# An adaLN attention and feed-forward block: a written-out table of steps for the first iterations, q taken first, scales by pointer, row sums on POOL, a staged passage to the feed forward

## The chip, the cores and the metric

The kernel runs on one core of a Trainium2 chip. A core has a matrix engine (TensorE, PE in the profile, its weight loads PEld), three elementwise engines (VectorE or DVE, ScalarE or ACT, GpSimd or POOL), and a queue engine (SyncE or SP) that issues the DMAs here. Each engine takes its instructions in program order and waits on semaphores for what the others produce. The metric is device time in microseconds, the median of several executions.

## What is computed

One transformer block with its modulation taken from a condition vector, in f32 inputs and outputs: 2048 rows of 512, 32 heads of 128, each attending to the last 512 rows of its cache, and a gated feed forward of width 1376.

```python
mod = (silu(c) @ w_mod).reshape(1, 6, 1, -1)       # sa, ca, ga, sb, cb, gb
h = layernorm(x) * (1 + ca) + sa
q = (h @ wq) per head; scores = q k^T * Dh**-0.5; o = softmax(scores) v   # k, v: last 512 rows
x = x + ga * (o @ wo)
h = layernorm(x) * (1 + cb) + sb
x = x + gb * ((gelu(h @ w_gate) * (h @ w_up)) @ w_down)
```

## The kernel before

Every f32 operand of a large product is split in a high and a low f16 part, and each product is made of three matmuls (high by high, high by low, low by high) that add up in one PSUM bank. So that f16 holds them, operands are scaled by their largest magnitude: `h_max` takes the maximum of a weight or cache tile on DVE (L239), `cross_a` and `cross_b` (L108, L117) bring it to all partitions with a transpose and a matmul, `h_scale` multiplies on POOL (L319) and `in_two` (L321) writes the high part on ACT and the low part on POOL. For some tiles `h_high` (ACT, L308) and `h_low` (DVE, L313) do both steps at once. `h_scalars` (L249) multiplies the inverse scales of a head, [128 x 1] each, into the factor of the exponential (L254, for wq and k) and the factor of the output (L257, for v and wo).

Queries come in 4 groups of 512 rows, heads in 16 groups of 2, which gives 128 iterations `it` of one head and one query group; 8 of them share two heads. The main loop `slot(i)` (L825) is a pipeline over iterations, written out in Python: slot i issues the scores of iteration i (`s_mm`, L440 to L442), its maxima (`s_max`, L448), exponentials (`s_exp`, ACT, L459 with the f16 copy L462), low parts and transposing DMAs (`s_low`, POOL L467 and SP L472), the value product of iteration i-2 (`pv`, L487 to L489), its evacuation (`o_high` L493, `o_low` L496) and the output product of iteration i-3 with its addition into `acc` (`wo_mm` L503, `wo_add` L515). A slot has two halves, and everything else is hung into named places of the halves: `at(half, f, ...)` puts a call in a list, and `hooks(half)` issues the list. Halves are counted 2i and 2i+1; n + 0.25 stands behind the first score product, n + 0.5 behind the maxima, n at the end of the first half, n + 1.25, n + 1.5 and n + 1 likewise in the second. `QS` holds the q products and `EV` their evacuation `q_high` (ACT, L428) and `q_low` (DVE, L431) out of the single PSUM bank psQ, issued one half slot later.

From head group 3 on q is made by a Strassen-like scheme of seven products for eight (`w_product`, L395), for which the normalised rows are added and subtracted: `t_full` (L357) adds high and low part to an f32 tile again, `t_sum` (L363) subtracts on POOL, `t_split` (L366) splits the result. Those steps are hung at halves 8 to 34.

Ahead of the loop (L544 to L613) the first query group is normalised: row statistics (`ln_stats`, DVE, with the reciprocal root by a power on POOL), the affine step on ACT (`ln_norm` L148), transposes on PE (`ln_pe` L160). `ln1_split` (L527) applies the modulation columns `cols` on the way out of PSUM and splits. The columns come from w_mod by eight DVE instructions and column matmuls (L554 to L561). `warm(n)` issues n transposes of the identity into an unused bank. The later three query groups are normalised and split in slots 0 to 3, by `ln_norm` and `ln1_chunk` hooks (L630 to L655), with the first heads' v and wo between them.

At the end of the loop `ff_cross` and `ff_scalars` (L792, L804) make the scales of the feed forward, `x1_mul` and `x1_add` form x + ga * attention of the first query group on POOL, `ln2_*` normalise it, and `fill` issues pieces of the first feed-forward products between the last slots. After the loop the feed forward runs over 4 query groups by 11 column tiles.

Tiles come from rings of named buffers: `raw` has 8, `h32` 3, `p32` 2, `q` 3; PSUM has one bank each for psO and psQ, two for psW and two pairs for the scores.

## Time and profile before

| | before |
|---|---|
| median of 3 runs | 1811.05 us (1810.65 to 1814.49) |
| profiled execution, its own time | 1813.38 us |
| span in that profile | 1811.6 us |
| mean granted TensorE clock | 0.984 |
| busy: PE, DVE, ACT, POOL | 95%, 72%, 59%, 58% |

The span runs from the first to the last instruction of the trace. A row of the timeline reads: start and duration in us, engine, line, operation, output and inputs with their shapes, how many, and in square brackets how long the engine idled before and on whom it waited. A row of the waits reads: who waits for whom, us in total, number of times, the longest. A row of a table of stretches reads: from and to, length, and for each engine busy us and instructions, then the granted clock, the share of DMA and GB/s. A row of groups reads: busy us and mean ns, then the idle time before the group; with three numbers and slashes it is minimum, median and maximum ns.

### The profile page before, as it was taken

What the parts mean: (1) busy time and instruction counts of PE and PEld (TensorE: products, weight loads), DVE (VectorE), ACT (ScalarE), POOL (GpSimd) and SP (SyncE); (2) the same over time, 40 slices, a digit from 0 to 9 for tenths busy, and PEclk for the clock granted to TensorE, in tenths of its full rate; (3) what the DMA queues carried; (4) which work ended last, traced back from release to release, by engine and by line L of the source; (5) the groups of instructions that cost most, each with busy time, mean ns of one, the idle gap of its engine ahead of it and who ended that gap; (6) DMA issues with size and microseconds to landing.
All of it is one profiled execution on the core that took longest, in us unless ns stands there. A gap on an engine that the chain in (4) does not pass through costs nothing. (4 is left out here: it accounts for less than half of the span.)

```text
span 1811.6 us, 23734 instructions
## 1 busy us (share of the span) xinstructions
PE 1721.7 (95%) x7950; PEld 790.7 (44%) x7950; DVE 1307.3 (72%) x2480; ACT 1077.1 (59%) x2016; POOL 1051.8 (58%) x826
## 2 busy tenths in 40 slices
PE   8688989999999999999999999999799899999998
PEld 5233434444444444444444444444344344444443
DVE  6678887878788888888887888888787746424222
ACT  3656757776767777776767676667577534121211
POOL 2557878687867767776767677676568800101010
PEclk8799999999999999999999999999999999999999
DMA  6346667687878777777768786767577731101000
GB/s 197 82 100 111 134 111 146 134 152 137 172 128 161 131 153 137 150 132 151 142 134 164 131 164 133 152 133 140 99 134 156 130 99 43 47 0 47 1 24 24
DMA packets 658954, 213.55 MB, mean 118 GB/s; under 512 B 580304, under 2 KB 640720, under 8 KB 658832
## 3 DMA queue, kind: packets, MB, share of 16 engines
q1 hardware_dynamic: 658832, 212.03, 58.6%
q8 instruction: 63, 1.03, 0.2%
q14 instruction: 59, 0.48, 0.1%
HBM read 65.14 MB, written 4.19 MB: 38 GB/s over the span
## 5 line engine op out<-in xcount | busy, mean ns | idle before, releaser
L467 POOL TENSOR_TENSOR pp<-p,pp 128x1024 f16<-128x1024 f32 x256 | 546.3, 2134 | 378.6 <-ACT pp L462 287.7
L459 ACT ACTIVATE p<-psS,st,es 128x512 f32<-128x512 f32 x512 | 393.2, 773 | 287.3 <-DVE st L450 279.6
L515 DVE SCALAR_TENSOR_TENSOR acc<-psW,st,acc 128x512 f32<-128x512 f32 x496 | 365.3, 741 | 24.1 <-PE psW L505 23.8
L448 DVE TENSOR_REDUCE st<-psS 128x2 f32<-128x1024 f32 x256 | 311.0, 1215 | 28.1 <-PE psS L442 27.1
L462 ACT ACTIVATE pp<-p 128x1024 f16<-128x1024 f32 x256 | 270.6, 1057 | 8.1
L503 PE MATMUL psW<-wo,oT 128*128 128x512 f16 x512 | 195.0, 381 | 23.5 <-DVE acc L515 22.1
L489 PE MATMUL psO<-pT,v 128*128 128x512 f16 x512 | 195.0, 381 | 5.7 <-POOL v L323 5.7
L440 PE MATMUL psS<-kT,q 128*128 128x512 f16 x512 | 197.2, 385 | 0.2 <-DMA kT<-k 0.2
L441 PE MATMUL psS<-kT,q 128*128 128x512 f16 x512 | 196.6, 384 | 0.0
L487 PE MATMUL psO<-pT,v 128*128 128x512 f16 x512 | 194.6, 380 | 2.0 <-ACT v L322 1.4
L442 PE MATMUL psS<-kT,q 128*128 128x512 f16 x512 | 196.3, 383 | 0.0
L504 PE MATMUL psW<-wo,oT 128*128 128x512 f16 x512 | 195.0, 381 | 0.0
L505 PE MATMUL psW<-wo,oT 128*128 128x512 f16 x512 | 194.6, 380 | 0.0
L488 PE MATMUL psO<-pT,v 128*128 128x512 f16 x512 | 194.6, 380 | 0.0
L1000 DVE SCALAR_TENSOR_TENSOR gl<-psS,ffs,gl 128x512 f32<-128x512 f32 (+1 forms) x44 | 33.0, 750 | 180.1 <-ACT gl L999 180.1
L999 ACT ACTIVATE gl<-psS,ffs 128x512 f32<-128x512 f32 (+1 forms) x44 | 30.2, 687 | 222.8 <-PE psS L989 222.8
L496 DVE SCALAR_TENSOR_TENSOR oT<-psO,oT 128x512 f16<-128x512 f32 x128 | 88.0, 687 | 40.2 <-ACT oT L493 39.9
L403 PE MATMUL psQ<-T,S 128*128 128x512 f16 x468 | 113.7, 379 | 2.9 <-DVE q L431 2.4
L239 DVE TENSOR_REDUCE mx<-raw 128x1 f32<-128x512 f32 x128 | 86.5, 679 | 41.5 <-DMA raw<-in_A_wq_dram 25.9
L493 ACT ACTIVATE oT<-psO 128x512 f16<-128x512 f32 x128 | 75.5, 590 | 58.5 <-PE psO L489 57.8
L459 ACT ACTIVATION_READ_ACCUMULATOR p<-psS,st,es 128x1 f32 x512 | 100.2, 196 | 0.0
L431 DVE SCALAR_TENSOR_TENSOR q<-psQ,q 128x512 f16<-128x512 f32 x49 | 33.7, 688 | 89.2 <-ACT q L428 89.2
(262 smaller groups left out, 3088.1 us busy)
## 6 DMA issues: line engine op xcount, KB each, us to landing
raw<-in_A_wq_dram SPq DMA_DIRECT2D x32, 256.0 KB, 3.3
raw<-in_A_k_cache_dram SPq DMA_DIRECT2D x32, 256.0 KB, 3.4
raw<-in_A_v_cache_dram SPq DMA_DIRECT2D x32, 256.0 KB, 3.4
...
pT<-pp SPq DMA_TRANSPOSE x512, 3.2
...
```

The source lines that it names most:

```text
L440: nc.tensor.matmul(p[:, j, :], q[:, 0, qs], k[:, 0, :], start=True, stop=False)
L441: nc.tensor.matmul(p[:, j, :], q[:, 0, qs], k[:, 1, :], start=False, stop=False)
L442: nc.tensor.matmul(p[:, j, :], q[:, 1, qs], k[:, 0, :], start=False, stop=True)
L448: nc.vector.tensor_reduce(st[:, 2 * b:2 * b + 2], PSS[it, b], op=OP.max, axis=AX.X, negate=True)
L459: nc.scalar.activation(p32[:, j, :], p[:, j, :], AF.Exp, bias=st[:, n:n + 1], scale=ES[head_qg(it)[0]][:, 0:1], accum_out=st[:, 4 + n:5 + n])
L462: nc.scalar.activation(pp[:, :, 0, :], p32, AF.Copy)
L467: nc.gpsimd.tensor_tensor(pp[:, :, 1, :], p32, pp[:, :, 0, :], op=OP.subtract)
L487: nc.tensor.matmul(po, vh, pT[:, t, :], start=(t == 0), stop=False)
L489: nc.tensor.matmul(po, v[:, 1, t * P:(t + 1) * P], pT[:, t, :], start=False, stop=(t == 3))
L503: nc.tensor.matmul(p, o[:, 0, ts], w[:, 0, :], start=True, stop=False)
L504: nc.tensor.matmul(p, o[:, 0, ts], w[:, 1, :], start=False, stop=False)
L515: nc.vector.scalar_tensor_tensor(a, p, r, a, op0=OP.mult, op1=OP.add)
```

## The change

The hooks and straight code of the beginning are replaced by one table, `PLAN`: each entry has a place (-1 for ahead of the loop, else a half), a step's name and its arguments. For `norm` and `chunk` the engine stands in the entry. In `slot`, `run(EV, ...)` moves ahead of the hooks of n + 0.25 and n + 1.25. In the setup the modulation sums come before the normalisation, the warm-up is 54 transposes and those between are gone; the two steps that make `cols` and its scale are taken apart. The negated mean times the root is formed by two POOL instructions when a group's statistics are complete. `h_scalars` and the feed forward's scalar steps use tensor_scalar with a pointer operand where they used scalar_tensor_tensor or tensor_tensor. The sums of `t_full` all run on POOL, and their order in the halves is new. The first head group's later loads and splits (`EARLY`) have other halves. At the end the scalar batch is cut in four, a memset moves to the setup, the scaling of gb moves to ACT, and the steps of the first feed-forward rows are hung one by one.

```diff
+PLAN = (
+    (-1, "stats", 1, 0), (-1, "stats", 1, 1), (-1, "max", "first", 0), (-1, "cols_add"), (-1, "cols_bound"),
+    (-1, "max", "first", 1), (-1, "warm", 0), (-1, "cols_scale"), (-1, "cross", "first", "a"),
+    (-1, "cross", "first", "b"), (-1, "stats", 1, 2), (-1, "chunk", 0, 0, "", "S", "Y"), (-1, "s_scale"),
+    (-1, "chunk", 0, 2, "", "V", "V"), (-1, "scalars", 0, "qk"), (-1, "high", "k", 0), (-1, "high", "wq", 0),
+    (-1, "chunk", 0, 1, "", "S", "Y"), (-1, "low", "wq", 0), (-1, "max", "second", 0),
+    (-1, "chunk", 0, 3, "", "S", "V"), (-1, "q", 0), (-1, "low", "k", 0), (-1, "turn", 0), (-1, "q_high", 0),
+    (-1, "max", "second", 1), (-1, "stats", 1, 3), (-1, "warm", 0), (-1, "cross", "second", "a"), (-1, "warm", 0),
+    (-1, "cross", "second", "b"), (-1, "warm", 0), (-1, "q_low", 0), (0.25, "norm", 1, 1, "V"),
+    (0.25, "high", "wq", 1), (0.25, "low", "wq", 1), (0.25, "high", "k", 1), (0.5, "norm", 1, 3, "S"),
+    (0.5, "norm", 1, 2, "S"), (0.5, "norm", 1, 0, "V"), (0, "low", "k", 1), (0, "q", 1), (0, "max", "later", 2),
+    (1.25, "q_high", 1), (1.25, "max", "later", 3), (1.25, "max", "later", 1),
+    (1.25, "chunk", 1, 1, "psW", "S", "Y"), (1.25, "q_low", 1), (1.5, "scalars", 1, "qk"), (1.5, "turn", 1),
+    (1.5, "chunk", 1, 3, "psO", "S", "Y"), (1.5, "chunk", 1, 0, "psQ", "V", "V"), (1.5, "stats", 2, 0),
+    (1.5, "stats", 2, 1), (1.5, "chunk", 1, 2, "psO", "S", "V"), (1.5, "stats", 2, 2), (1, "stats", 2, 3),
+    (1, "max", "later", 0), (1, "stats", 3, 0), (2.25, "cross", "later", "a"), (2.25, "norm", 2, 2, "V"),
+    (2.25, "norm", 2, 3, "S"), (2.25, "cross", "later", "b"), (2.5, "norm", 2, 0, "S"), (2.5, "scale", "v", 0),
+    (2.5, "scale", "wo", 0), (2.5, "norm", 2, 1, "V"), (2, "stats", 3, 1), (2, "chunk", 2, 0, "psO", "S", "Y"),
+    (2, "stats", 3, 2), (3.5, "chunk", 2, 1, "psW", "V", "V"), (3.5, "split", "v", 0), (3, "scalars", 0, "vo"),
+    (3, "stats", 3, 3), (4.25, "chunk", 2, 2, "psW", "V", "Y"), (4.25, "high", "v", 1), (4.5, "split", "wo", 0),
+    (4.5, "chunk", 2, 3, "psW", "S", "Y"), (4, "norm", 3, 2, "V"), (4, "norm", 3, 1, "S"), (5.5, "norm", 3, 0, "S"),
+    (5, "norm", 3, 3, "V"), (5, "chunk", 3, 1, "psW", "S", "Y"), (5, "low", "v", 1), (6.25, "scale", "wo", 1),
+    (6.25, "scalars", 1, "vo"), (6.25, "chunk", 3, 0, "psW", "S", "Y"), (6.5, "chunk", 3, 2, "psW", "S", "Y"),
+    (6, "split", "wo", 1), (7.5, "chunk", 3, 3, "psW", "V", "V"),
+)
+EARLY = {("wq", 0): (1, 5, 9, 10), ("wq", 1): (1, 5, 10, 11), ("k", 0): (2, 5, 10, 11, 12), ("k", 1): (2, 5, 9, 13, 15),
+         ("v", 0): (3, 6, 13, 14), ("wo", 0): (4, 9, 15, 16), ("v", 1): (6, 8, 15, 19), ("wo", 1): (8, 11, 19, 22)}
-    EARLY = {("wq", 0): (1, 4, 9, 10), ("wq", 1): (1, 5, 10, 11), ("k", 0): (2, 6, 10, 11, 12), ("k", 1): (2, 7, 12, 13, 15),
-             ("v", 0): (5, 7, 14, 15), ("wo", 0): (6, 8, 15, 16), ("v", 1): (7, 9, 16, 20), ("wo", 1): (8, 10, 17, 22)}
...
     def ln_stats(key, src, j):
...
+            if key in range(NQG) or key == ("2", 0):
+                nm = NMR[key] = small(base, 4, 4, "nmr")
+                nc.gpsimd.tensor_tensor(nm, MV[key][:, :, 0], RS[key], op=OP.mult)
+                nc.gpsimd.tensor_scalar(nm, nm, -1.0, 1.0, op0=OP.mult, op1=OP.mult)
...
-            nc.vector.scalar_tensor_tensor(ES[h][:, 0:1], IV.pop(("wq", h)), sc1[:, 1:2], IV.pop(("k", h)),
-                                           op0=OP.mult, op1=OP.mult)
+            nc.vector.tensor_scalar(ES[h][:, 0:1], IV.pop(("wq", h)), IV.pop(("k", h)), sc1[:, 1:2],
+                                    op0=OP.mult, op1=OP.mult)
...
-    warm(62)
+    warm(54)
     for j in range(4):
         ln_stats(0, acc[j], j)
+    for j in (1, 0):
+        for k in range(NC):
+            mod_sum(j, k)
     for j in range(4):
         ln_norm(0, acc[j], acc[j], j, S_)
...
+    ln1_turn(0, 0, where[0])
+    mod_cols(1)
+    for c in (1, 2, 3):
+        ln1_turn(0, c, where[c])
+    mod_cols(0)
...
-            at(n + 1, t_full, p, c, "12", V)
-            at(n + 2, t_sum, p, c, "11", "12", "11")
-            at(n + 2, t_full, p, c, "22", V)
-            at(n + 3, t_split, p, c, "T1", "11")
-            at(n + 3, t_sum, p, c, "12", "22", "12")
-            at(n + 4, t_sum, p, c, "22", "22", "11")
+            at(n, t_full, p, c, "12", Y)
+            at(n + 1, t_sum, p, c, "11", "12", "11")
+            at(n + 1, t_full, p, c, "22", Y)
+            at(n + 2, t_split, p, c, "T1", "11")
+            at(n + 2, t_sum, p, c, "12", "22", "12")
+            at(n + 3, t_sum, p, c, "22", "22", "11")
             at(n + 4, t_split, p, c, "T3", "12")
-            at(n + 5, t_full, p, c, "21", V)
+            at(n + 4, t_full, p, c, "21", Y)
             at(n + 5, t_sum, p, c, "21", "21", "22")
-            at(n + 5, t_split, p, c, "T2", "22")
+            at(n + 6, t_split, p, c, "T2", "22")
...
     at(s + 3, ff_cross)
-    at(s + 5, ff_scalars)
+    for part in range(4):
+        at(s + (7, 10, 12, 14)[part], ff_scalars, part)
...
         when(i, s_mm, 0)
+        run(EV, n - 1)
         hooks(n + 0.25)
-        run(EV, n - 1)
...
-        n = e + 8 + (j + 1) // 2
-        at(n, x1_mul, 0, j, nc.gpsimd)
-        at(n, x1_add, 0, j, nc.gpsimd)
-        at(n + 1, ln2_stats, 0, j)
-        at(e + 12, ln2_norm, 0, j)
+        at(e + 8 + j, x1_mul, 0, j, nc.gpsimd)
+        at(e + 8 + j, x1_add, 0, j, nc.gpsimd)
+        at(e + 10 + j, ln2_stats, 0, j)
+        at(e + 14.5, ln2_norm, 0, j)
...
-    for c, (a, b) in enumerate(((13, 14.5), (14.5, 14), (14, 15.5), (15.5, 15))):
+    for c, (a, b, d) in enumerate(((15.5, 15, 16.25), (15, 16.25, 16.5), (16.5, 16, 17.25), (16, 17.25, 17.5))):
         at(e + a, ln2_chunk, 0, c, nc.vector if c % 2 else nc.scalar)
-        at(e + a, ln2_high, 0, c)
-        at(e + b, ln2_low, 0, c, nc.gpsimd)
+        at(e + b, ln2_high, 0, c)
+        at(e + d, ln2_low, 0, c, nc.gpsimd)
...
-    for half, n in ((16, 3), (17, 3), (18, 2), (19.5, 1), (19, 3), (20.5, 1), (20, 1), (21.5, 1), (21, 1)):
+    for half, n in ((17, 2), (18.5, 1), (18, 3), (19.5, 3), (19, 3), (20.5, 1), (20, 1), (21.5, 1), (21, 1)):
         at(e + half, fill, n, False)
```

In a chunk's entry the last two letters are the engine of the affine step (S: ACT writes the f32 tile and the high part; V: ACT writes the high part, DVE the f32 tile) and that of the low part (V DVE, Y POOL).

More of the change, by code (lines that the diff above doesn't have):

```diff
@@ L566, in adaln_block, with mod_sum, mod_cols @@
     nc.gpsimd.memset(plus[:, 4:8], 0.0)
+    MM = {}
+    def mod_sum(j, k):
+        if k == 0:
+            MM[j] = right.tile([P, N], F32, name="mm", tag="p32", bufs=2)
+            nc.vector.tensor_scalar_mul(MM[j], wm[j][:, 0, :], silu[:, 0:1])
+        else:
+            nc.vector.scalar_tensor_tensor(MM[j], wm[j][:, k, :], silu[:, k:k + 1], MM[j], op0=OP.mult, op1=OP.add)
+    def mod_cols(j):
+        for f in range(NC):
+            n = 4 * (1 - j) + f
+            nc.tensor.matmul(two[:, 0, n:n + 1], MM[j][:, f * P:(f + 1) * P], ones[:, 0:1], start=True, stop=True)
+    warm(54)
+    for j in range(4):
+        ln_stats(0, acc[j], j)
+    for j in (1, 0):
+        for k in range(NC):
+            mod_sum(j, k)
+    for j in range(4):
+        ln_norm(0, acc[j], acc[j], j, S_)
+    where = (bank("psO"), bank("psW", 2), bank("psW", 2), tail_[:, 0, :])
+    ln1_turn(0, 0, where[0])
[3 more added lines that the diff above has]
+    mod_cols(0)
     first = [("wq", 0), ("k", 0)]
@@ L611, in adaln_block, with cols_add, cols_bound @@
-    h_turn(1)
-    for j in (2, 3):
-        ln_stats(1, acc[4 + j], j)
+    def cols_add():
+        nc.vector.tensor_tensor(cols[:, 0:8], two[:, 0, 0:8], plus, op=OP.add)
+        nc.vector.tensor_tensor(sq, cols[:, 0:8], cols[:, 0:8], op=OP.mult)
+    def cols_bound():
+        nc.tensor.matmul(two[:, 0, 16:24], ones, sq, start=True, stop=True)
+        nc.vector.tensor_reduce(sc1[:, 2:3], two[:, 0, 16:24], op=OP.add, axis=AX.X)
+        nc.vector.tensor_scalar(sc1[:, 3:4], sc1[:, 2:3], 1e-30, 2.0 / HQS ** 2, op0=OP.max, op1=OP.mult)
+        nc.gpsimd.tensor_tensor(sc1[:, 0:1], sc1[:, 3:4], eps_t[:, NC:NC + 1], op=OP.pow)
@@ L623, in hooks, with chunk @@
             f(*a)
[L626 to L627 removed]
+    def chunk(qg, c, tag, full, low):
+        if qg:
+            ln1_turn(qg, c, tail_[:, 1, :] if tag == "tail" else bank(tag, 2 if tag == "psW" else 1))
         ln1_split(qg, c, full, low)
[L630 to L636 removed]
@@ L651, in adaln_block, with cross @@
-    for c, (half, full, low) in enumerate(((3.5, V, V), (3.5, S_, Y), (4.25, V, V), (4.25, S_, Y))):
-        at(half, ln1_chunk, 2, c, "psW", full, low)
-    for c, (half, tag, full, low) in enumerate(((5, "psO", S_, V), (5, "psW", V, V), (7, "psO", S_, Y),
-                                                (7, "psW", V, Y))):
-        at(half, ln1_chunk, 3, c, tag, full, low)
+    def cross(which, part):
+        w = {"first": first, "second": second, "later": later}[which]
+        pt = None if w is later else two[:, 1, :]
+        if part == "a":
+            h_cross_a(w, mxs[w is later], pt)
+        else:
+            h_cross_b(w, pt)
@@ new lines, in largest @@
+    def largest(which, i):
+        w = {"first": first, "second": second, "later": later}[which]
+        h_max(w[i], mxs[w is later], i)
+    STEP = {"max": largest, "cols_add": cols_add, "cols_bound": cols_bound, "cols_scale": cols_scale, "s_scale": s_scale,
+            "warm": warm, "cross": cross, "chunk": chunk, "high": h_high, "low": h_low, "scale": h_scale,
+            "split": h_split, "turn": h_turn, "scalars": h_scalars, "q": lambda it: q_proj(it, 0, NC), "q_high": q_high,
+            "q_low": q_low, "load": load_raw,
+            "stats": lambda qg, j: ln_stats(qg, acc[4 * qg + j], j),
+            "norm": lambda qg, j, e: ln_norm(qg, acc[4 * qg + j], acc[4 * qg + j], j, {"V": V, "S": S_}[e])}
@@ L773, in adaln_block @@
     nc.gpsimd.memset(mff, 0.0)
+    mxf = small(base, 8, 1, "mxf")
+    nc.gpsimd.memset(mxf, 0.0)
     FM = {}
@@ L792, in ff_cross @@
     def ff_cross():
[L793 to L794 removed]
+        m = mxf
         for i in range(2):
```

176 lines of the change are left out of this document (55 added, 121 removed).

## The prediction, made before the changed kernel was run

> **What bounds the kernel now.** I read the page's first part, then PE's waits over the whole span, then a table of stretches cut at the first score matmul (L440) of chosen slots.
>
> ```profile
> PE 1721.7 (95%) x7950; PEld 790.7 (44%) x7950; DVE 1307.3 (72%) x2480; ACT 1077.1 (59%) x2016; POOL 1051.8 (58%) x826
> PE psQ L385 <- DVE q L431: 24.1, 10, 8.5
> 26.10:34.27 8.17, 6.54 (x15) 1.74 (x15) 7.59 (x16) 3.71 (x6) 1.37 (x1) 0.58 0.23 53
> 34.27:105.38 71.11, 48.27 (x197) 22.39 (x197) 48.04 (x97) 44.57 (x78) 37.54 (x31) 0.80 0.39 79
> 105.38:273.37 167.99, 153.63 (x688) 68.28 (x687) 138.20 (x253) 101.96 (x195) 125.13 (x93) 0.97 0.60 113
> 105.38:351.07 245.69, 229.19 (x1035) 102.25 (x1034) 198.55 (x369) 158.44 (x304) 182.50 (x138) 0.98 0.65 124
> 351.07:1273.31 922.24, 903.97 (x4180) 408.16 (x4179) 769.80 (x1491) 659.84 (x1266) 667.90 (x515) 1.00 0.75 145
> 1273.31:1316.14 42.83, 32.64 (x142) 14.17 (x142) 30.36 (x65) 19.61 (x38) 23.37 (x21) 0.96 0.50 88
> 1335.85:1407.50 71.65, 71.65 (x335) 32.50 (x333) 53.19 (x105) 53.67 (x102) 54.36 (x40) 1.00 0.78 151
> 1407.50:1480.00 72.50, 63.76 (x289) 28.59 (x288) 47.15 (x85) 33.65 (x58) 35.04 (x27) 0.98 0.49 98
> ```
>
> PE is 95% busy, but that share hides where it is not. The stretch at 1335.85 is PE without a gap: 71.65 us for 335 matmuls, **0.214 us each**. Holding every stretch against that price gives what PE loses there (a little too much for the short transposes): slots 0 to 3 (34.27 to 105.38) 71.1 - 197 x 0.214 = **28.9 us**; slots 4 to 24 245.7 - 221.5 = **24.2**; slots 25 to 112 922.2 - 894.5 = **27.7**; slots 113 to 115 42.8 - 30.4 = **12.4**; the passage into the feed forward, 1407.5 to 1480, 72.5 - 61.8 = **10.7**. Ahead of slot 0 lie 34.3 us of loading and setting up. So some 104 us in the loops, and most of the 34 ahead of them, are waits and half clock (0.80 granted in slots 0 to 3). Everything the change touches lies in one of these places.
>
> **The change part by part.** Gains are negative. Sums go against the profiled execution, 1813.38 us (its span 1811.6 and 1.8 around it), 2.3 above the median 1811.05; the final figure is moved to the median.
>
> *A. Ahead of slot 0.*
>
> ```profile
> 9.99 0.16 DVE L146 SCALAR_TENSOR_TENSOR nmr<-mv,rs 128x4 f32<-128x4 f32 x1 [1.50 <-POOL rs L139]
> 19.21 0.95 PE L561 MATMUL psS<-ones,mm 128*128 128x1 f32 x8
> 20.27 0.17 DVE L572 TENSOR_TENSOR cols<-psS,plus 128x8 f32<-128x8 f32 x1 [3.41 <-PE psS L561]
> 24.38 0.20 DVE L586 TENSOR_SCALAR cols<-cols,sc 128x8 f32<-128x8 f32 x1
> 28.73 10.04 SPq L292 DMA_TRANSPOSE kT<-k  x2
> kT<-k SPq DMA_TRANSPOSE x32, 3.2
> 34.27 0.39 PE L440 MATMUL psS<-kT,q 128*128 128x512 f16 x1
> ```
>
> DVE now waits 1.50 us for POOL before it starts the modulation sums, and the column matmuls (L561) stand behind warm-up blocks of 24 and 10 matmuls. After: the negated mean goes to POOL, which idles there, the sums start at 8.5, and the columns follow the transposes at once; I get them at 17.4 instead of 20.16. The chain from cols to its scaling took 4.3 us (20.27 to 24.58) with two row statistics and the cross step inside; alone it is some 2.8. The scaled columns are there at about 20.2, 4.4 earlier. What is late next: ACT has the four chunks and both high parts (about 6.4 us, to 26.6), then DVE has k's low part (to 28.2), then the k transpose lands 3.2 after its issue (median, last but one row), 31.4. It was issued at 28.73 before and hid behind q; now it ends the stretch. First score at 31.6, not 34.27: **-3**, bounds -6 (all of the 4.4 and some of the idle ACT) and +1.
>
> The clock in the row 26.10 to 34.27 is 0.58 although a warm-up block ran just ahead of it, so removing the blocks (62 to 54 at first, 24, 10, 4 and 10 to none) costs q 0 nothing new. The Trainium skill, "TensorE: Matmul & The Clock Gate", section "What's actually happening", says that full speed takes about 3.4 us of sustained work; by it the six first scores could also run at half rate, an estimated 1.3 us, and this term would be -1.7.
>
> *B. Slots 0 to 3.*
>
> ```profile
> 57.49 2.93 ACT L153 ACTIVATE acc<-acc,nmr,rs 128x512 f32<-128x512 f32 x4 [7.02 <-DVE nmr L146]
> 60.32 0.57 ACT L428 ACTIVATE q<-psQ 128x512 f16<-128x512 f32 x1
> 61.67 0.58 PE L385 MATMUL psQ<-B,A 128*128 128x512 f16 x1 [8.54 <-DVE q L431]
> 43.91 0.63 ACT L534 ACTIVATE B<-h 128x512 f16<-128x512 f32 x1
> 44.62 1.16 POOL L538 TENSOR_TENSOR B<-h,B 128x512 f16<-128x512 f32 x1 [0.36 <-ACT B L534]
> L467 POOL TENSOR_TENSOR pp<-p,pp 128x1024 f16<-128x1024 f32 x256 | 546.3, 2134 | 378.6 <-ACT pp L462 287.7
> L459 ACT ACTIVATE p<-psS,st,es 128x512 f32<-128x512 f32 x512 | 393.2, 773 | 287.3 <-DVE st L450 279.6
> L462 ACT ACTIVATE pp<-p 128x1024 f16<-128x1024 f32 x256 | 270.6, 1057 | 8.1
> ```
>
> The worst wait is plain: q's evacuation on ACT (60.32) stood behind four normalisations (2.93 us) that waited 7.02 for DVE, and PE stood 8.54. With EV ahead of the hooks, q is taken first. No engine was full (48.0 DVE, 44.6 ACT of 71.1), so order is what is bought. Counting the table for these slots: ACT eight exponentials at 2 x 0.773 + 1.057 and a tenth for reading the sums 21.8, eight chunks at 0.77 + 0.63 11.2, four half chunks 3.1, six norms at 2.93 / 4 4.4, high parts (six of 0.63, one larger) 4.1, six of q and o at 0.57 3.5: 48 us. DVE, counted the same way, 46. POOL eight L467 17, eight chunk lows at 1.16 9.3, the rest 9: 35. PE 42. ACT becomes the floor: 48. Laying the instructions in queue order by hand gives 52 us for the four slots; my walk leaves out handoffs, so I add a tenth: 57, **-14**, bounds -21 (ACT without a gap) and 0 (waits only move).
>
> *C. Slots 4 to 24: row sums, EARLY.*
>
> ```profile
> L361 DVE TENSOR_TENSOR tf<-B 128x512 f32<-128x512 f16 x8 | 9.8, 1225 | 0.0
> L361 DVE TENSOR_TENSOR tf<-T 128x512 f32<-128x512 f16 x4 | 3.2, 810 | 0.0
> L361 POOL TENSOR_TENSOR tf<-B 128x512 f32<-128x512 f16 x4 | 5.2, 1288 | 0.0
> 264.36 0.63 ACT L322 ACTIVATE T<-tf 128x512 f16<-128x512 f32 x1 [2.32 <-POOL tf L364]
> ```
>
> Twelve sums leave DVE (9.8 + 3.2 = 13.0 us) and cost POOL 12 x 1.29 = 15.5. In slots 4 to 17 POOL goes from 125 to some 140 us, against 14 x 10.36 = 145 for PE (48 matmuls a slot): 97%. That alone would be no gain. But the consumers move: T3 is split two half slots after its sum and T2 three, where it was one, so ACT stops standing before POOL (the 2.32 above) with q behind it, and DVE's sums no longer sit ahead of q's low part. Nine of PE's ten waits for q, 24.1 - 8.5 = 15.6 us, are here. The new EARLY steps spread POOL's scaling. I take a bit more than a third of 24.2: **-9**, bounds +4 (POOL's lag reaches PE) and -18.
>
> *D. Scales by pointer, slots 25 to 112.*
>
> ```profile
> 1022.60 2.97 DVE L254 SCALAR_TENSOR_TENSOR es<-iv,sc 128x1 f32<-128x1 f32 x2
> 1023.41 2.14 POOL L467 TENSOR_TENSOR pp<-p,pp 128x1024 f16<-128x1024 f32 x1
> 1026.88 0.38 PE L503 MATMUL psW<-wo,oT 128*128 128x512 f16 x1 [1.34 <-DVE acc L515]
> PE psW L503 <- DVE acc L515: 13.0, 11, 1.3
> L254 DVE SCALAR_TENSOR_TENSOR es<-iv,sc x32: 167/920/2164, 31.6 to 1274.6; 128x1 f32<-128x1 f32 x32
> L450 DVE TENSOR_SCALAR st<-st,es x512: 202/209/216, 39.0 to 1439.7; 128x1 f32<-128x1 f32 x171
> L477 DVE TENSOR_SCALAR st<-st,es x128: 228/246/1347, 85.3 to 1461.6; 128x4 f32<-128x4 f32 x128
> ```
>
> Once in eight slots two one-column products (L254) take 2.97 us; the second ends as POOL's L467 ends (1025.55). wo's accumulation queues behind, and PE waits 1.3 us: 13.0 us in eleven places of this stretch (the fourth row is PE's waits from 351.07 to 1273.31). L254 has two SBUF inputs, minimum 0.167, median 0.920. The new form is that of L450: one column, pointer scalar, 512 times and never over 0.216. **-13**, bounds -13 and 0.
>
> The Trainium skill, "SBUF — State Buffer", section "SBUF: two separate sides", says that a DVE instruction with two SBUF inputs, or in a two-port mode, and a POOL instruction exclude each other for a whole instruction; the trace agrees (2.97 against 0.167). "VectorE: DVE Perf Modes", section "The perf-mode tier table", gives f32 tensor_scalar in SBUF a doubled mode, which by the first rule would still be held: that is rival 2, and L477, held to 1.347 at four columns, speaks for it; L450 at one column against it.
>
> *E. Feed-forward scales, slots 113 to 115.*
>
> ```profile
> 1288.18 0.11 POOL L794 MEMSET mxf<- 128x8 f32 x1
> 1288.91 0.27 PE L110 MATMUL psO<-ident,mxf 128*8 128x128 f32 x1 [4.86 <-DVE mxf L799]
> 1302.01 2.09 DVE L806 COPY ffs<-av 128x3 f32<-128x3 f32 x1
> 1418.84 0.58 PE L503 MATMUL psW<-wo,oT 128*128 128x512 f16 x1 [3.69 <-DVE acc L515]
> ```
>
> A 0.11 us memset in POOL's queue held DVE and then PE for 4.86; it moves to the setup. The scalar batch that opens at 1302.01 (twelve DVE instructions in a row) becomes four parts on four half slots, with pointers, and the scaling of gb goes to ACT (one pass like L459's 0.77, in ACT's idle time). 128x3 may still be held 2 us once. With the L254 wait of slot 113, of 12.4 I take **-9**, bounds -4 and -11.
>
> *F. Passage to the feed forward.* x1's multiplies and adds come one a half slot and statistics two later, so the 3.69 goes. Against it, no fill stands in slot 128's first half, and 4 fewer pieces (12 matmuls, 2.6 us of PE) ahead of the last head's pv. **-2**, bounds -6 and +3.
>
> At nothing: the memset, plus and buffer counts (SBUF only), q's order argument (same order), the loads that move on SP's queue (v and wo of the next heads, one or two half slots ahead of transposes; DMA is 0.39 busy there).
>
> Sum: -3 - 14 - 9 - 13 - 9 - 2 = -50: 1763 for a profiled execution, **1761** at the median.
>
> **The rivals.**
> 1. *POOL becomes the bound in slots 0 to 24* (97% above, in-order, p32 in two buffers so that ACT's exponential waits for POOL two half slots later). For: the 125.13 of 168. Against: its consumers have more room. C is lost and half of B: 1777.
> 2. *The pointer form is still held by POOL*: D is lost: 1774.
> 3. *The table doesn't do what it says*, its stalls only move: A and B are lost: 1778.
> 4. *Slower*: POOL's instructions stretch under the denser start; L361 shows 1.29 mean for 1.16 of work. At 1.45 times its 140 us, POOL needs 203 us for slots 4 to 17, 35 more than now, and slots 0 to 3 keep their 71: with A, D, E and F still gained (-27) that is 1819. It decides from a stretch of about 1.4; nothing in the trace is near it for long.
>
> **How the numbers follow.** Forecast 0.60, rival 1 0.17, rival 2 0.08, rival 3 0.09, rival 4 0.04, none of it adding up to anything 0.02. 0.2% (3.6 us) is what a measurement can tell here. Only 4 is slower, so faster 0.94, same 0.02, slower 0.04. The terms' own ends give 1736 and, for one or two lost, 1774 to 1787; range **1742 to 1787**.
>
> **What would show it.** First score near 31.6; slot 4's score near 88; no wait over 4 us of psQ for q; pointer scales at 0.2 us and no 1.3 us waits of psW once in eight slots; no wait before the cross of mxf; POOL 0.9 or more busy in slots 4 to 17 without PE waiting for it. Wrong if POOL's s_low falls more than a slot behind its scores, if kT lands after 34, or if PE stands between 1440 and 1480 before pv.

## The result and the profile after

| | after | before, on the same chip |
|---|---|---|
| median | 1759.73 us (4 runs, 1756.95 to 1764.70) | 1812.77 us (4 runs, 1810.65 to 1817.35) |
| ratio | 0.971, 95% interval 0.968 to 0.974 | |
| profiled execution: its own time, span | 1760.75 us, 1758.9 us | 1813.38 us, 1811.6 us |
| mean granted TensorE clock | 0.990 | 0.984 |

The forecast was 1761, the range 1742 to 1787. The sum came out, but that is luck in part: A and D gave 8.7 us less than forecast, the other four terms 11.4 us more. Cut at the first score matmul of the same slots as in the prediction (L470 now, L440 before), the two profiled executions compare like this:

| stretch | before, us | after, us | difference | predicted |
|---|---|---|---|---|
| A: ahead of slot 0 | 34.27 | 34.58 | **+0.3** | -3 |
| B: slots 0 to 3 | 71.11 | 51.26 | **-19.9** | -14 |
| C: slots 4 to 24 | 245.69 | 236.05 | -9.6 | -9 |
| D: slots 25 to 112 | 922.24 | 914.65 | **-7.6** | -13 |
| E: slots 113 to 115 | 42.83 | 31.16 | -11.7 | -9 |
| F: slot 116 to the end | 495.46 | 491.20 | -4.3 | -2 |
| sum | 1811.60 | 1758.90 | -52.7 | -50 |

From the profile after: first the busy line of the page, then the table of stretches (from and to, length, busy us and instructions of PE, PEld, DVE, ACT, POOL, granted clock, DMA share, GB/s).

```profile
PE 1704.3 (97%) x7894; PEld 784.1 (45%) x7894; DVE 1274.8 (72%) x2459; ACT 1082.0 (62%) x2021; POOL 1061.8 (60%) x846
```

```profile
34.58:85.84 51.26, 42.23 (x197) 20.28 (x197) 43.58 (x87) 44.17 (x79) 32.89 (x29) 0.94 0.47 98
85.84:244.16 158.32, 150.68 (x689) 67.50 (x686) 128.24 (x245) 102.71 (x198) 135.47 (x104) 0.99 0.67 124
321.89:1236.54 914.65, 902.96 (x4179) 408.97 (x4179) 753.79 (x1492) 662.12 (x1266) 666.90 (x516) 1.00 0.75 146
1236.54:1267.70 31.16, 30.55 (x142) 13.71 (x142) 25.64 (x53) 20.73 (x41) 23.87 (x20) 1.00 0.71 127
```

Slots 0 to 3 have the same 197 matmuls as before, but PE's own time for them fell from 48.27 to 42.23 us and the granted clock rose from 0.80 to 0.94: some 6 of B's 19.9 us are PE's own time at the higher clock. The prediction did not name that part, though its count of 42 us for PE in these slots has it in. Slots 113 to 115 are full (30.55 of 31.16). Slots 4 to 17, where rival 1 saw POOL at 97%, have it at 135.47 of 158.32, 86%. Slots 25 to 112 still leave 11.7 us (914.65 - 902.96), although the waits that the prediction priced there are gone, as the groups (minimum, median and maximum ns) and PE's waits of that stretch (us in total, times, longest) show:

```profile
L283 DVE TENSOR_SCALAR es<-iv,sc x32: 221/263/269, 27.7 to 1237.2; 128x1 f32<-128x1 f32 x32
```

```profile
PE psO L517 <- DVE mr L145: 3.6, 1, 3.6
PE psO L152 <- DVE oT L526: 3.2, 6, 0.7
```

The wait of psW for acc (13.0 us in eleven places) has no row any more. In its place stands one wait of 3.6 us for `mr`, of the cross step. The timeline after, ahead of slot 38, shows where it comes from (here and below, rows of other instructions in between are left out):

```profile
457.86 2.12 POOL L497 TENSOR_TENSOR pp<-p,pp 128x1024 f16<-128x1024 f32 x1
...
459.61 4.82 DVE L507 TENSOR_SCALAR st<-st,es 128x4 f32<-128x4 f32 x1
459.95 1.26 POOL L757 TENSOR_TENSOR gb<-gb,raw 128x512 f32<-128x512 f32 x1
461.18 2.11 POOL L497 TENSOR_TENSOR pp<-p,pp 128x1024 f16<-128x1024 f32 x1
463.26 1.14 POOL L352 TENSOR_TENSOR k<-raw,k 128x512 f16<-128x512 f32 x1
...
464.67 0.58 PE L517 MATMUL psO<-pT,v 128*128 128x512 f16 x1 [3.57 <-DVE mr L145]
```

L507 is the product of four reciprocals with the head's factor, 128 x 4, usually 0.23 us. Here it starts 0.37 us before the end of a POOL instruction (457.86 + 2.12 = 459.98), lasts 4.82 and ends at 464.43, as the third POOL instruction behind that one ends (463.26 + 1.14 = 464.40). The cross step behind it is late, and PE with it; slot 38 takes 16.0 us where it took 10.8 before. This is 5.2 of the 5.4 us by which D fell short; the other slots of the stretch together fall by 12.8 us (911.5 to 898.7).

And the beginning, in the timeline of before (two rows) and of after:

```profile
8.31 0.18 DVE L135 BATCH_NORM_AGGREGATE mv<-bnst 128x2 f32<-128x6 f32 x1
...
10.19 2.93 ACT L153 ACTIVATE acc<-acc,nmr,rs 128x512 f32<-128x512 f32 x4 [6.90 <-DVE nmr L146]
```

```profile
9.34 0.18 DVE L168 BATCH_NORM_AGGREGATE mv<-bnst 128x2 f32<-128x6 f32 x1
...
10.03 1.53 POOL L172 TENSOR_TENSOR rs<-ve,eps_t 128x4 f32<-128x4 f32 x1
11.64 0.67 POOL L175 TENSOR_TENSOR nmr<-mv,rs 128x4 f32<-128x4 f32 x1
...
12.40 0.30 POOL L176 TENSOR_SCALAR nmr<-nmr 128x4 f32<-128x4 f32 x1
12.74 2.93 ACT L182 ACTIVATE acc<-acc,nmr,rs 128x512 f32<-128x512 f32 x4 [9.62 <-POOL nmr L176]
...
21.42 0.17 DVE L614 TENSOR_TENSOR cols<-psS,plus 128x8 f32<-128x8 f32 x1 [2.79 <-PE psS L592]
...
27.02 0.61 PE L415 MATMUL psQ<-T,A 128*128 128x512 f16 x1 [2.18 <-ACT A L337]
...
31.09 1.34 SPq L321 DMA_TRANSPOSE kT<-k  x1
...
34.06 0.59 PE L152 MATMUL psS<-dg,ones 8*128 8x8 f32 x2 [0.62 <-DVE dg L147]
34.58 0.61 PE L470 MATMUL psS<-kT,q 128*128 128x512 f16 x1
```

From the view of the DMAs after, the same transfer (the last number is us from issue to landing):

```profile
kT<-k SPq DMA_TRANSPOSE x1, 3.1
```

A is a sum of three. The statistics end 1.03 us later (8.31 + 0.18 against 9.34 + 0.18), because rows of x land later in this execution (DVE waits 1.85 us for them, 0.82 before). From there to the first normalisation on ACT it is 3.22 us, was 1.70: **+1.52**. From the normalisation to the first score it is 21.84 us (12.74 to 34.58), was 24.08: **-2.24**. Together +0.31. At the end of this stretch k's transpose lands at about 34.2 (31.09 and 3.1), but PE does not wait for it: the first score follows without a pause behind the cross step of the second head's scales (L152), which stands behind q's twelve matmuls on PE.

### The profile page after: what moved, and what is told of

The parts are those of the page before. It is cut to its first block, busy times and chain, and to the rows that moved or that the text cites. A ratio compares the mean times of both kernels' runs of the same rounds, so it can differ in the third digit from the quotient of the medians.

```text
span 1758.9 us, 23632 instructions
## 1 busy us (share of the span) xinstructions
PE 1704.3 (97%) x7894; PEld 784.1 (45%) x7894; DVE 1274.8 (72%) x2459; ACT 1082.0 (62%) x2021; POOL 1061.8 (60%) x846
## 4 chain that ended last, share of the span: by engine, by line
PE 66%; DVE 12%; ACT 9%; POOL 3%; DMA 3%; issue 3%; SPq 3%; ACTq 0%; DVEq 0%; POOLq 0%
PE psQ L433 9%; PE psS L1010 4%; PE psS L1011 4%; PE psS L1012 4%; PE psS L470 4%; PE psS L472 4%; PE psO L519 4%; PE psO L517 4%; PE psO L518 4%; PE psS L471 4%; PE psW L533 4%; PE psW L534 4%; PE psW L535 4%; ACT p L489 4%; DVE st L478 3%
## 5 line engine op out<-in xcount | busy, mean ns | idle before, releaser
L497 POOL TENSOR_TENSOR pp<-p,pp 128x1024 f16<-128x1024 f32 x256 | 545.3, 2130 | 333.9 <-ACT pp L492 240.4
L470 PE MATMUL psS<-kT,q 128*128 128x512 f16 x512 | 195.1, 381 | 1.0 <-DMA kT<-k 1.0
```

The lines of the kernel that those rows point to most:

```text
L470: nc.tensor.matmul(p[:, j, :], q[:, 0, qs], k[:, 0, :], start=True, stop=False)
L497: nc.gpsimd.tensor_tensor(pp[:, :, 1, :], p32, pp[:, :, 0, :], op=OP.subtract)
```

## The experiments

Each run was timed beside the kernel before on its chip. Total times of the changed kernel spread over some 8 us (1756.95 to 1764.70), so edits worth less than about 4 us are read from the stretches of the traces, where a stretch that an edit doesn't touch mostly repeats within some 2 us either way (the exceptions come below). The stretches are those of one profiled execution each.

| run | median, us | ratio to before, 95% interval | first score | slots 0-3 | 4-24 | 25-112 | 113-115 |
|---|---|---|---|---|---|---|---|
| before | 1812.77 | | 34.27 | 71.11 | 245.69 | 922.24 | 42.83 |
| after | 1759.73 | 0.9707 (0.9677-0.9738) | 34.58 | 51.26 | 236.05 | 914.65 | 31.16 |
| e1, before with pointer forms | 1799.08 | 0.9892 (0.9870-0.9915) | 34.03 | 72.94 | 244.07 | 910.43 | 40.66 |
| e2, after without them | 1777.46 | 0.9784 (0.9764-0.9804) | 33.03 | 50.29 | 239.31 | 927.60 | 33.27 |
| e3, twelve sums on DVE | 1763.57 | 0.9703 (0.9685-0.9721) | 34.27 | 51.07 | 240.91 | 916.30 | 31.15 |
| e4, q behind the hooks | 1762.68 | 0.9700 (0.9683-0.9716) | 32.38 | 52.52 | 238.45 | 913.99 | 31.16 |
| e5, feed-forward scalars in one batch | 1768.58 | 0.9750 (0.9735-0.9764) | 33.61 | 51.25 | 237.54 | 912.46 | 39.38 |
| e6, one k split later | 1762.69 | 0.9715 (0.9699-0.9731) | 31.21 | 51.25 | 244.79 | 916.52 | 31.15 |
| e7, first nmr on DVE | 1757.64 | 0.9692 (0.9677-0.9706) | 30.88 | 51.52 | 236.97 | 914.10 | 31.15 |
| e8, four columns always | 1760.59 | 0.9704 (0.9688-0.9721) | 33.30 | 51.09 | 237.05 | 914.82 | 31.31 |
| e9, old steps in slots 0 to 3 | 1775.32 | 0.9779 (0.9763-0.9796) | 32.85 | 67.08 | 235.99 | 916.28 | 31.15 |
| e10, four columns, iteration 36 | 1761.43 | 0.9701 (0.9674-0.9729) | 34.20 | 49.75 | 237.40 | 916.61 | 31.15 |
| e11, PE kept busy ahead of q | 1749.26 | 0.9632 (0.9611-0.9652) | 32.98 | 53.84 | 234.65 | 904.02 | 31.15 |
| e12, four columns, iteration 35 | 1759.15 | 0.9701 (0.9684-0.9717) | 33.99 | 51.46 | 241.41 | 912.52 | 31.16 |

### The pointer forms (term D): e1 and e2

e1 takes the kernel before and changes only this; e2 takes the changed kernel and puts the old forms back.

```diff
-            nc.vector.scalar_tensor_tensor(ES[h][:, 0:1], IV.pop(("wq", h)), sc1[:, 1:2], IV.pop(("k", h)), ...)
+            nc.vector.tensor_scalar(ES[h][:, 0:1], IV.pop(("wq", h)), IV.pop(("k", h)), sc1[:, 1:2], ...)
```

> The kernel before with nothing but the two products of inverse scales written as tensor_scalar with a pointer operand. Theory (one-column tensor_scalar is not held by POOL, and the 1.3 us waits of PE once in eight slots come from it): L254 at 0.2 to 0.3 us in all 32 places, the eleven waits of psW for acc in slots 25 to 112 gone (13.0 us), slots 25 to 112 in 909 us instead of 922, and with slots 9, 17 and 113 some 15 us in all, so near 1797. Rival (the wait only moves to the next thing DVE is late with, as the changed kernel's -7.6 us in that stretch could be read): 922 minus 3 to 8 us, near 1804.

> The changed kernel with the two products of inverse scales as scalar_tensor_tensor again. Theory: slots 25 to 112 lengthen by 12 to 13 us from 914.7 and the waits of psW for acc are back at 1.0 to 1.35 us once in eight slots; slots 4 to 24 lengthen by 2 to 4 us; near 1775. Rival (other parts of the change hide them by now): under 5 us, near 1764.

Alone, the forms give 1799.08 against 1816.77; undone, they cost 1777.46 against 1759.73. Slots 25 to 112 fall by 11.8 us in e1 and rise by 12.95 in e2. The groups and the waits of e2 in that stretch have the old picture back:

```profile
L283 DVE SCALAR_TENSOR_TENSOR es<-iv,sc x22: 719/1080/2164, 323.1 to 1168.2; 128x1 f32<-128x1 f32 x22
```

```profile
PE psW L533 <- DVE acc L545: 13.2, 11, 1.3
```

So the price in the prediction (13.0) was that of the mechanism: e2 is the clean test, since slot 38 takes 16.0 us without the old forms and 16.2 with them. But e1 has the new stall as well, without anything else of the change. Its timeline at slot 38:

```profile
488.12 4.71 DVE L477 TENSOR_SCALAR st<-st,es 128x4 f32<-128x4 f32 x1
...
491.64 1.16 POOL L323 TENSOR_TENSOR k<-raw,k 128x512 f16<-128x512 f32 x1
```

Slot 38 takes 16.1 us there, so the rest of e1's stretch falls by 17.1, some 4 us more than the waits that were priced; where those come from stays open. With the old forms and the old order slot 38 took 10.8; in e1 another instruction of DVE meets POOL's train. e2, with the old forms in the new order, has the stall too (4.81 us). So more than one arrangement leads into it, and it is not the price of the pointer forms alone.

### The order in slots 0 to 3 (term B): e4 and e9

e4 puts the evacuation behind the hooks again, in both halves. e9 leaves it ahead and gives the steps of slots 0 to 3 their old halves, order and engines, with head 1's wq and k ahead of the loop.

```diff
-        run(EV, n - 1)
         hooks(n + 0.25)
+        run(EV, n - 1)
...
-    (0.25, "norm", 1, 1, "V"), (0.25, "high", "wq", 1), ... (7.5, "chunk", 3, 3, "psW", "V", "V"),
+    (-1, "scale", "k", 1), (-1, "scalars", 1, "qk"), (-1, "high", "wq", 1), (-1, "low", "wq", 1),
+    (-1, "split", "k", 1), (-1, "turn", 1), (0.25, "q", 1), (0, "q_high", 1), (0, "q_low", 1),
+    (0.5, "norm", 1, 0, "V"), ... (2.25, "norm", 2, 0, "S"), ... (7, "chunk", 3, 3, "psW", "V", "Y"),
```

> The changed kernel with the evacuation of q behind the hooks again, as it was before. Theory (the order of the table's entries does most of slots 0 to 3, but q behind cross and norm of slot 1 costs what it cost): slots 0 to 3 lengthen from 51.3 by 5 to 9 us, with a wait of psQ for q of 3 us or more. Rival (the table has already moved what stood in front of q, so the order of q and hooks is worth little): under 2 us.

> The changed kernel with the steps of slots 0 to 3 in the places and the order they had before (head 1's wq and k done ahead of the loop, q of iteration 1 evacuated in the same half, norms, statistics, scales and chunks as before); q's evacuation ahead of the hooks, the pointer forms and the rest stay. Theory, the order in the table carries term B: slots 0 to 3 go from 51.3 to 62 to 70 us, and the time rises by 10 to 19 us (to 1770 to 1779). Rival, the place of the evacuation did it, since the worst wait before (8.54 us) was a q behind four normalisations: slots 0 to 3 stay under 57 us and the time within 4 us.

e4: slots 0 to 3 take 52.52, 1.3 us more, and the total cannot be told from the changed kernel's; the rival there was right. e9: 67.08 us and 1775.32, inside the theory's bounds. Its stretch and PE's waits in it:

```profile
32.85:99.93 67.08, 49.05 (x198) 21.85 (x197) 46.71 (x91) 42.67 (x76) 34.13 (x32) 0.80 0.42 86
```

```profile
PE psQ L401 <- DVE q L447: 5.9, 2, 3.4
PE psO L505 <- POOL v L338: 4.8, 2, 3.6
```

The 8.54 us wait behind the four normalisations is gone in e9 too, and what it gave is small: 71.11 to 67.08 at most, since e9 keeps the rest of the change. The other 15.8 us are the table's as a whole: places, order and engines were not taken apart. With the old steps PE waits in long pieces for q and for v, and the clock granted is 0.80 again, 49.05 us for nearly the same matmuls that take 42.23 at 0.94. So the cost of a wait here is the wait and the half clock after it.

### Row sums and EARLY (term C): e3 and e6

```diff
-            at(n, t_full, p, c, "12", Y)
+            at(n, t_full, p, c, "12", V)
...
-    ("k", 1): (2, 5, 9, 13, 15),
+    ("k", 1): (2, 5, 9, 14, 15),
```

(e3 above, likewise for "22" and "21"; e6 below.)

> The changed kernel with twelve of the sixteen sums of high and low part on DVE instead of POOL, at their new places. Theory (the gain of slots 4 to 24 comes from taking the sums off DVE, where they wait for POOL in front of q's low part): slots 4 to 24 lengthen from 236.1 by 4 to 8 us, and single sums on DVE last 1.2 to 2.5 us. Rival (the gain comes from the new places alone, and POOL is only made fuller): within 2 us of 236.1, or shorter.

> The changed kernel with one half of one step moved: the second k of head group 1 is split at half 14 instead of 13. Theory (slot 7 keeps its 16 us because ACT's high part of that k waits for the transposing DMA of the k before it, which reads the only k16 buffer, and q's evacuation stands behind): slot 7 from 16.1 to 11 to 12 us, so -4 to -5 in slots 4 to 24. Rival (another instruction of that half stands late as well): slot 7 stays over 14, or slot 8 takes the wait.

e3: slots 4 to 24 take 4.9 us more in its trace, but the whole time, 1763.57 against 1759.73, does not settle it. The stretch of slots 4 to 17 in e3:

```profile
85.34:248.70 163.36, 150.43 (x689) 66.96 (x687) 139.09 (x257) 102.77 (x198) 126.87 (x93) 1.00 0.61 120
```

POOL's 135.47 us become 126.87 and DVE's 128.24 become 139.09; the engine that has the sums is 85 or 86% busy either way, so these shares don't say why DVE is the worse place for them. The longer stretch fits the theory, and is no proof of its size. The rest of C, the later places of the splits and the new `EARLY` as a whole, no run took apart.

e6 tested slot 7 (16.1 us in the changed kernel). There PE waits 3.79 us for q, the split of a k tile on ACT standing ahead behind its transposing DMA. Moving the split half a slot later takes that wait away and makes a larger one, DVE's and then PE's (waits of the two engines around slots 7 and 8):

```profile
DVE mx L268 <- DMA raw<-in_A_k_cache_dram: 8.5, 1, 8.5
```

```profile
PE psW L533 <- DVE acc L543: 5.8, 1, 5.8
```

Slots 7 and 8 take 17.9 and 12.5 us, from 16.1 and 10.8. DVE, in order, stands before a load that lands later; that it does so because its buffer is released later was not followed up. A later split is worse; an earlier one was not tried. Most of the rest of e6's rise in slots 4 to 24 is slot 17 (15.6 us), which the edit does not touch; it comes back below.

### The scalars of the feed forward (term E): e5

```diff
-        at(s + (7, 10, 12, 14)[part], ff_scalars, part)
+        at(s + 5, ff_scalars, part)
...
+        nc.gpsimd.memset(mxf, 0.0)
```

> The changed kernel with the feed forward's scalars as one batch again, two half slots after their cross step, and the memset of their maxima back in POOL's queue just ahead of it; the pointer forms, and gb on ACT, stay. Theory (the stall came from the place, a memset behind POOL's work and twelve DVE instructions in a row): slots 113 to 115 lengthen from 31.2 by 6 to 9 us. Rival (it came from the forms that POOL held, the copy's 2.09 us first): under 3 us.

Slots 113 to 115 rise from 31.16 to 39.38, 8.2 us, and the time to 1768.58. The timeline of e5 shows the memset's part, as it was before:

```profile
1247.62 0.10 POOL L810 MEMSET mxf<- 128x8 f32 x1
...
1248.34 0.31 PE L143 MATMUL psO<-ident,mxf 128*8 128x128 f32 x1 [4.24 <-DVE mxf L815]
```

A 0.10 us instruction in the queue of a busy engine costs PE 4.24 us; the other 4 of the 8.2 us lie with the batch, which this run did not take apart further. The last 3.5 of E's 11.7 us, which e5 leaves in place, were not tested either (pointer forms, gb on ACT).

### The beginning (term A): e7 and e11

e7 forms the first group's negated mean on DVE, ahead of the modulation sums. e11 fills PE's pauses ahead of q with transposes of the identity.

```diff
+            if key == 0:
...
+                nc.vector.scalar_tensor_tensor(nm, MV[key][:, :, 0], -1.0, RS[key], op0=OP.mult, op1=OP.mult)
...
-    (-1, "max", "first", 1), (-1, "warm", 0), (-1, "cols_scale"),
+    (-1, "max", "first", 1), (-1, "warm", 6), (-1, "cols_scale"),
...
-    (-1, "cross", "first", "b"), (-1, "stats", 1, 2),
+    (-1, "cross", "first", "b"), (-1, "warm", 14), (-1, "stats", 1, 2),
```

> The changed kernel with the first query group's negated mean on DVE again, ahead of the modulation sums. Theory (in the changed kernel the power and the two products on POOL are held by DVE's modulation sums, power 1.53 instead of 1.03 us, product 0.67 instead of 0.20, so the normalisation starts 3.4 us after the statistics' end): ACT's normalisation starts about 1.7 us after the last statistics, as before, and the columns and the first score come 1 to 1.5 us earlier. Rival (w_mod's arrival or PE's half clock sets the columns): the columns within 0.5 us.

> The changed kernel with 6 transposes of the identity between the statistic of the columns and their scaling, and 14 behind the first cross step, where PE waits before q of iteration 0. Theory, the half clock is what is left ahead of slot 0: q's twelve matmuls run at up to 0.21 us each instead of 0.43, and from the start of the first normalisation on ACT to the first score it takes 19.5 to 20.8 us instead of 21.8. Rival, as the prediction had it, the blocks buy nothing: 21.5 us or more, since this stretch is too short to raise the clock or the blocks delay what stands behind them.

In e7's timeline the statistics end at 7.83 and the normalisation starts at 9.54:

```profile
7.65 0.18 DVE L168 BATCH_NORM_AGGREGATE mv<-bnst 128x2 f32<-128x6 f32 x1
...
9.54 2.93 ACT L185 ACTIVATE acc<-acc,nmr,rs 128x512 f32<-128x512 f32 x4 [6.39 <-DMA wm<-in_w_mod_dram]
```

1.71 us, as before the change (1.70); the eleven traces that have these steps on POOL (after, e2 to e6 and e8 to e12) take 2.45 to 3.28. So the move to POOL costs 0.7 to 1.6 us. e7's first score, 30.88, is 3.70 us earlier than that of the changed kernel: 1.51 of it is this step, 1.69 is the earlier end of the statistics, which wait for x, and 0.50 the rest (e6, without this edit, has 31.21). In the total (1757.64) so little cannot be told.

e11 gave the largest gain of all, 10 us, and not where it was looked for. Its timeline:

```profile
23.66 3.18 PE L553 MATMUL psQ<-ident 128*128 128x128 f32 x14
...
26.90 0.38 PE L415 MATMUL psQ<-T,A 128*128 128x512 f16 x1
...
29.79 1.33 SPq L321 DMA_TRANSPOSE kT<-k  x1
...
30.46 0.60 ACT L458 ACTIVATE q<-psQ 128x512 f16<-128x512 f32 x1 [2.14 <-PE psQ L417]
...
32.98 0.38 PE L470 MATMUL psS<-kT,q 128*128 128x512 f16 x1 [1.00 <-ACT A L337]
```

The clock theory was right about q: its matmuls last 0.38 us where they lasted 0.61 and 0.63, and all twelve are done 3.5 us after the first, not 6.2. The Trainium skill, "TensorE: Matmul & The Clock Gate", section "What's actually happening", gives about 3.4 us of sustained work for full speed. The trace of e11 agrees: the two blocks make 1.52 and 3.18 us of it, and the granted clock from q's first matmul to the end of its last is 1.00, where it was 0.50 (27.02 to 33.22). But from the normalisation (10.69) to the first score it takes 22.29 us, no less than 21.84. q's high part is in SBUF at 31.06, and PE stands for 1.00 us before the score at 32.98: k's transposing DMA, issued at 29.79, takes 3.1 us to land. So in e11 k's transpose ends this stretch. In the changed kernel PE's own queue did, 0.35 us behind that landing, so a faster q could give no more than those 0.35 us. The rival's number (21.5 or more) came true, its first reason (that the clock would not rise) did not.

The gain is in slots 25 to 112 (904.02, 10.6 less; slots 0 to 3 take 2.6 more), with slot 38 at 12.3 and no other slot from 31 on over 11 us, where after has seven. Nothing is edited there. Counted from the start of slot 36, DVE's and POOL's instructions in the traces of after and e11 agree within 0.03 us, one by one, up to a load that ACT waits for:

```profile
456.90 0.72 ACT L756 ACTIVATE raw<-raw,silu 128x512 f32<-128x512 f32 x1 [0.39 <-DMA raw<-in_w_mod_dram]
```

```profile
456.30 0.72 ACT L756 ACTIVATE raw<-raw,silu 128x512 f32<-128x512 f32 x1 [1.06 <-DMA raw<-in_w_mod_dram]
458.66 1.29 POOL L757 TENSOR_TENSOR gb<-gb,raw 128x512 f32<-128x512 f32 x1
459.01 0.97 DVE L507 TENSOR_SCALAR st<-st,es 128x4 f32<-128x4 f32 x1
460.19 2.15 DVE L147 TENSOR_SCALAR dg<-ident,mr 8x8 f32<-8x8 f32 x1
```

(after, then e11.) A row of w_mod lands 0.67 us later within the slot in e11: ACT waits 1.06 us for it, not 0.39. So o and everything behind it on DVE come 0.67 us later against POOL, whose L757 starts at the same moment. L507 now comes after L757 has started, gets through in POOL's pause after it (0.97), and the next DVE instruction that can be held is held 2.15 us by one POOL instruction. That is the 3.7 us of slot 38. Of the other 6.9, PE's waits for o ahead of the cross steps once in eight slots are 3.7 (4.8 in after, 1.1 in e11); why these went was not traced. All four runs of e11 lie between 1744.1 and 1750.3, so it repeats; what shifts the load was not tried, so that the added transposes as such bring the gain is not shown.

### The held product: e8, e10, e12

L283 and L480 show that one column is not held. e8 does the four-column product as four one-column ones in every iteration, e10 in iteration 36 alone, e12 in iteration 35 alone.

```diff
-        nc.vector.tensor_scalar_mul(st[:, 8:12], st[:, 8:12], RV[head_qg(it)[0]])
+        if it == 35:
+            for n in range(8, 12):
+                nc.vector.tensor_scalar_mul(st[:, n:n + 1], st[:, n:n + 1], RV[head_qg(it)[0]])
+        else:
+            nc.vector.tensor_scalar_mul(st[:, 8:12], st[:, 8:12], RV[head_qg(it)[0]])
```

> The changed kernel with the product of the four reciprocal sums and the output factor written as four one-column products instead of one of four columns. Theory (the four-column form is held by POOL, one column is not): no such product over 0.3 us, slot 38 from 16.0 to 10.8 us, the slots of 11.1 to 11.6 two before each multiple of eight to 10.8, together -9 to -12 us in slots 25 to 112. Rival (0.45 us more DVE work a slot, 57 us in all, makes DVE late for psW): no gain in that stretch, or a loss of up to 10 us.

> The changed kernel, but in iteration 36 alone (its product by the head's factor lasted 4.82 us in slot 38) the four-column product is done as four one-column products. Theory, the hold is all there is to slot 38: that slot goes from 16.0 to about 10.8 us, slots 25 to 112 from 914.7 to about 909.5, the time falls by some 5 us. Rival, the wait moves, as where all iterations had four columns: slot 38 falls, but the slots after it take it back, and slots 25 to 112 stay above 913 us.

> The changed kernel with four one-column products in iteration 35 alone. The run before took iteration 36 and missed: the trace shows that the product that lasts 4.7 to 4.8 us is issued two slots after its iteration, at the end of slot 37, so it is that of iteration 35. Theory, the hold at the end of slot 37 is all there is to slot 38: that slot goes from 16.0 to 11 or 12 us (the cross step's 8x8 product may still be held some 2 us), slots 25 to 112 from 914.7 to 910 or 911, and the time falls by 4 to 5 us. Rival, the hold comes from the moment at which a load lands and moves on with it: slot 38 falls but slots 25 to 112 stay above 913 us, or, the other way, the small waits of slots 46 to 110 go with it and they come to 904 to 907, as where slots 0 to 3 were changed.

In e8 the group of the product reads:

```profile
L508 DVE TENSOR_SCALAR st<-st,es x512: 202/205/216, 70.8 to 1410.9; 128x1 f32<-128x1 f32 x171
```

Never over 0.216 us, and the stall of slot 38 is gone (11.0 us). That shows what is held and what is not. It bought nothing: other slots lengthen (39, 47, 55, 63, 71, 79, 95, 103 and 111 go from at most 10.82 to 11.2), and the sum is 914.82. That fits the rival, three more instructions a slot being some 0.35 us of DVE.

e10 missed: the product is issued two slots after its iteration, and the held one, at the end of slot 37, is that of iteration 35. So e10 is nearly the changed kernel again, and its 1761.43 tells how far such a time repeats. e12 took the right one, and the hold went to the next instruction that can be held. Its timeline:

```profile
465.17 1.28 POOL L761 TENSOR_TENSOR gb<-gb,raw 128x512 f32<-128x512 f32 x1
...
465.67 4.00 DVE L147 TENSOR_SCALAR dg<-ident,mr 8x8 f32<-8x8 f32 x1
...
468.47 1.18 POOL L352 TENSOR_TENSOR k<-raw,k 128x512 f16<-128x512 f32 x1
```

L147 ends at 469.67 with POOL's last one (469.65). Slot 38 takes 14.6 instead of 16.0, slots 25 to 112 take 912.52, and the time, 1759.15, is the changed kernel's. Neither a time 4 to 5 us shorter nor the other way, 904 to 907, came; the stretch lies 0.5 us under the rival's bound of 913. So the product is not the whole cause: out of the way, it left its place to the next instruction that can be held. POOL's row without a pause is what these long holds share, but it is not enough to make one. Mostly the DVE instruction gets in as soon as the POOL instruction that runs has ended, though POOL's next one follows at once. The timeline after, at the end of slot 40:

```profile
495.20 1.15 POOL L352 TENSOR_TENSOR wo<-raw,wo 128x512 f16<-128x512 f32 x1
...
495.54 0.85 DVE L507 TENSOR_SCALAR st<-st,es 128x4 f32<-128x4 f32 x1
...
496.32 1.16 POOL L352 TENSOR_TENSOR q<-h,q 128x512 f16<-128x512 f32 x1
```

L507 ends at 496.39, 0.04 us after the first L352, and the second does not hold it. Of the 43 products of 128 x 4 and 8 x 8 that last over 0.5 us in that trace, 29 end so, 10 end with one POOL instruction and a pause, 3 go past one boundary that comes within 0.12 us of their start, and one, slot 38, goes past three. What makes slot 38 different no run shows.

Slot 17 has such a long hold too, in the profiled execution of e6 and of e12 but not of after. In e6:

```profile
234.07 5.68 DVE L507 TENSOR_SCALAR st<-st,es 128x4 f32<-128x4 f32 x1
...
237.57 2.13 POOL L497 TENSOR_TENSOR pp<-p,pp 128x1024 f16<-128x1024 f32 x1
```

It goes past the end of the POOL instruction that runs and through four more, 5.68 us, and ends with the last of them (239.70), although POOL goes on at 239.67. Slot 17 takes 15.6 us in e6 and 15.8 in e12, 10.8 in after. Both profiled executions are the slowest of their kernel's runs (1767.72 of 1761.55 to 1767.72, and 1763.60 of 1756.23 to 1763.60), which a hold that comes in some executions and not in others would explain; that every slow run has it was not shown.

## Why the prediction was right, and where not

**A, ahead of slot 0, failed** at the step "the negated mean goes to POOL, which idles there". POOL had no work of its own, but the same edit starts DVE's modulation sums, which have two inputs in SBUF, at that moment. From the statistics to the normalisation it takes 0.7 to 1.6 us longer than in e7, on the path: after, the power lasts 1.53 us where it lasted 1.03 (before, and in e7), and the two new steps 0.67 and 0.30. In other traces it is the new steps that stretch (e2: 1.03, then 0.63 and 0.70). That DVE's sums hold POOL there is argued from this; e7 moves the product and delays the sums at once, so it does not separate the two. The gain behind it was 2.24 us, where the prediction counted on 3 for the score and 4.4 for the columns; the columns came at 21.4, not 17.4, because their matmuls stand behind transposes that wait for ACT. Its last link came close: k's transpose, named for 31.4, lands at about 34.2, which is past the 34 that the prediction gave as a sign of being wrong, and the first score stands 0.35 us behind it, in PE's own queue.

The Trainium skill's rule in that place ("TensorE: Matmul & The Clock Gate", section "What's actually happening"), full speed only after some 3.4 us of sustained work, was weighed and given 1.3 us against the change. The six first scores do take 2.81 us (34.58 to 37.39, granted 0.50), where six at 0.214 take 1.28; but that price, 1.5, lies in slot 0, so in B. The 6.2 us of q ahead of them, the last 4.6 without a pause, had not raised the clock, so here 3.4 us of work were not enough. That blocks of transposes bring q nothing, as the prediction read from the 0.58 of before, is not so: in e11 they bring it full speed, which here is worth 0.35 us at most.

**B** had the right place and sign; its size was 19.9 for 14, near the outer bound of 21. The step that was argued as the worst, q behind four normalisations, carries 1.3 us in the new order (e4) and at most the 4.0 that e9 keeps; the table carries 15.8. Counting busy time and walking the queues by hand gave 52 us for the four slots, which was nearly exact (51.26). The tenth added for handoffs was too much. The walk left handoffs out and the measured time has them in, so that the two meet so closely is luck in part.

**C** came out (9.6 for 9), but its size had been taken as a share of a loss and not added up, so the match is luck in part. By e3 about half of it may be the sums' engine. POOL stayed at 86%, so rival 1 did not decide; the sums take 1.155 us each, not the 1.29 of the row that was used.

**D**: the 13.0 us of waits went, as e1 and e2 show from both sides. What the sum lacked is another instruction that POOL can hold: the four-column product, which the prediction quoted at 1.347 us as evidence for a rival, and which now cost 5.2 us in slot 38. Either part alone brings that about: the pointer forms in the old order (e1), or the new order with the old forms (e2). **E** was under-sized by 2.7 (11.7, of which e5 gives back 8.2). **F** is 2.3 better than predicted; the 3.69 us wait is gone (PE's longest between 1350 and 1430 is 1.51 now), and no run took the rest apart.

Rivals 2, 3 and 4 are out: one column with a pointer, L283, never passes 0.269 us (four columns are still held); the stalls of B did not move on into C, which fell by 9.6 itself; POOL's instructions did not stretch (its L497 has a mean of 2130 ns, 2134 before).
